# Packed attention and a channel mixer on one core: half of the packs are made between the mixer's products

## The chip, the cores and the metric

The kernel runs on one core of a Trainium2 chip. TensorE (PE) multiplies matrices and writes its results to PSUM; VectorE (DVE), ScalarE (ACT) and GpSimd (POOL) work elementwise; SyncE (SP) issues all transfers of this kernel. Each engine takes its instructions from its own queue, in order, and waits on semaphores for the others. The metric is the time of one execution in microseconds (us); lower is better.

## The reference

There are 8 batches of 8 heads with 576 tokens and 64 channels. Each head has 32 learned "pack" queries `p`. First the packs attend to the tokens, then the tokens attend to the packs:

```python
p_packed = sm_attn(p, k, v)              # 32 x 64 per head: "the packs"
x = sm_attn(q, p_packed, p_packed)       # 576 x 64 per head
# heads side by side: x is (8, 576, 512)
u = x + (x.transpose(0, 2, 1) @ U @ V).transpose(0, 2, 1)
out = u + np.maximum(u @ w_ch1, 0) @ w_ch2
```

`sm_attn` is a softmax attention with scale 1/8, the row maximum subtracted and 1e-9 added to the sum. `U` (576 x 32), `V`, `w_ch1` (512 x 2048) and `w_ch2` (2048 x 512) come as 64-bit floats, everything else as 32-bit.

## The kernel before

**Numbers.** A float32 matrix is split into a high part and a rest (`fp32r` tiles with names that end in h and l, or hi and lo), and three products stand for one (`mm3`, L74 to L78). `float32_of` (L67 to L71) turns 64-bit words into float32: one ACT and four VectorE instructions on a 128 x 512 tile.

**The packs are folded into w1.** Since the packs of a batch are the values of the second attention, `u @ w1` becomes "attention weights times (packs @ w1)". The products packs @ w1 are written to DRAM (`wsr` for batches 0 to 3, `wsc` for batches 4 to 7) and read back in pieces of 256 columns (`load_wt`, `split_wt`).

**First stage.** A unit is one batch and half of its heads (four). For all 16 units, in rounds (the loop over `i`, L479), the kernel loads k, v and p, turns k with VectorE (`a_split`, the 128 x 1152 transposition of L101) and p into a block-diagonal tile `bdp`, multiplies (`a_scores`), takes the maximum over all 576 tokens and the exponential (`a_softmax`), turns the weights with TensorE (`a_turn`) and multiplies them with v (`a_pack`): one product per 128 tokens, 128 rows (4 heads x 32 packs) by 256 columns (4 heads x 64), of which only the four diagonal blocks are used; ScalarE scales these by the reciprocal of the sum into `ppall`. In the same rounds `some_w1` converts and splits the 16 chunks of w1, `a_pairs` and `fold` make the products of batches 0 to 3 with w1, and steps of `attention(0)` are taken. A planner sets the order of the instructions in this stage, by program order and by what is ready. After the loop come the remaining folds, the rest of `attention(0)`, the first pieces of folded weights, the first chunk of w2, and the first two steps of `attention(1)`.

**The batches.** From L531 on the order is as written. For each batch b and each of 16 column blocks kt (NK = 16, 128 columns each): `gemm1(kt)` (12 products into `h_ps0` and `h_ps1`; ScalarE writes relu into `hh` and `hjh`, VectorE the rests `hl` and `hjl`), then `gemm2(kt - 1)` (12 products into the four `o` tiles), then at even kt `load_wt` and `split_wt`, in batch 0 `split_w2`, `load_w2` and `convert_w2`, then from batch 1 on the steps of `later`, which fold batches 4 to 7 into `wsc` (`twice` and `heads` turn their packs, `load`, `convert`, `split_heads`, `product` handle one chunk of w1), and then one step of the list `steps`, the second attention of the batch that follows. `h_ps0` and `h_ps1` have one buffer each: the next `gemm1` waits until `hl` and `hjl` are written. Each pair of batches has a joint product for its last 64 tokens (`joint`).

**Second attention.** `attention(b, res)` is a list of 16 steps, one per kt: `blocks` writes the packs into the block-diagonal tile `bdq` (L167) and splits it into `bqh` (ACT, L170) and `bql` (POOL, L171); `turn_q` and `split_q` turn and split q (`nat`, `natT`, `nhi`, `nlo`, one buffer each); then scores, softmax, `tokens` (into two `vt` buffers), `mix1` and `mix2`. Its first step is taken at kt 12 two batches ahead of its own, the others one per kt in the batch ahead of its own. PSUM for all this, and for `heads` and `product`, is the pool `psT` with two buffers.

The change and the prediction touch the first stage's units (L288 to L379, the loop at L479), `attention` (L157), `later` (L551) and the loop over batches (from L687).

Of the kernel before, what the change touches and what calls it, by code (L numbers as in the profile page):

```python
# [8 lines left out]
F32 = mybir.dt.float32  # L9
F32R = mybir.dt.float32r  # L10
I32 = mybir.dt.int32
AF = mybir.ActivationFunctionType
ALU = mybir.AluOpType
AX = mybir.AxisListType
# [5 lines left out]
def packed_attention_mixer_kernel(  # L20
# [23 lines left out]
    nc = tc.nc  # L44
    B, H, S, D = q.shape
# [4 lines left out]
    P = 128  # L50
    NB = S // 32
    SM = 512
    NK = DF // P
    NU = 2 * B
# [217 lines left out]

    res = {}
# [11 lines left out]
    UN = [(b, g) for b in range(B) for g in range(2)]  # L285
    ua = {}
# [8 lines left out]

    def a_load_v(u):
        b, g = UN[u]
        gh = slice(4 * g, 4 * g + 4)
        vt = pipe.tile([P, 5, 4 * D], F32, name="vt", tag="vt", bufs=2)
        nc.sync.dma_start(out=vt[:, :4].rearrange("p h x -> p (h x)").rearrange("p (h x) -> p h x", h=4),  # L300
                          in_=v[b, gh, :SM].rearrange("h (p k) d -> p h (k d)", k=4))
        nc.sync.dma_start(out=vt[:64, 4].rearrange("p (h d) -> p h d", h=4),
                          in_=v[b, gh, SM:].rearrange("h p d -> p h d"))
        ua[u]["v"] = vt
# [47 lines left out]
    def a_pack(u):  # L352
# [10 lines left out]
        if b < B // 2:  # L363
            ua[u]["twice"] = sA.tile([P, 2, D], F32, name="twice", bufs=1)
            nc.scalar.copy(ua[u]["twice"], ppall[:, b, g].unsqueeze(1).to_broadcast([P, 2, D]))
# [95 lines left out]
    a_load_v(0)  # L461
# [17 lines left out]
    for i in range(NU + 3):  # L479
# [4 lines left out]
        if i + 1 < NU:  # L484
            a_load_v(i + 1)
# [4 lines left out]
        if i > 1:  # L490
            some_w1()
        if i < NU:
            a_softmax(i)
        if i >= 5 and first and i not in (16, 17):
            first.pop(0)()
# [5 lines left out]
        if 0 <= i - 3 < NU // 2:  # L501
            a_pairs(i - 3)
        if 6 < i < 13:
            some_w1()
# [21 lines left out]
    for _ in range(2):  # L526
        steps.pop(0)()
# [162 lines left out]
    folds[0][0]()  # L690
    folds[0][1]()
    for b in range(B):
# [3 lines left out]
        for kt in range(NK):  # L696
# [3 lines left out]
            if done and kt % 2 == 0 and kt > 0:  # L700
                pr, cc = done.pop(0)
                folds[pr][5](cc)
# [20 lines left out]
            if b > 0 and kt > 0:  # L723
# [5 lines left out]
                elif kt % 2 == 1:  # L729
# [6 lines left out]
                    if rest and kt < NK - 1:  # L736
                        pr, cc = rest.pop(0)
                        folds[pr][2](cc)
                        held.append((pr, cc))
            if steps:  # L740
                steps.pop(0)()
            if kt == 1:
                cur.blocks()
# [41 lines left out]
```

## Time and profile before

| | us |
|---|---|
| median of 3 runs (lowest, highest) | 874.68 (874.37, 875.54) |
| the profiled execution | 876.01 |
| its span, first to last instruction | 874.2 |
| TensorE busy in the span | 826.7 (95%) |
| VectorE busy | 512.6 (59%) |
| ScalarE busy | 374.0 (43%) |
| GpSimd busy | 258.6 (30%) |
| read from and written to DRAM | 71.5 and 26.2 MB, 112 GB/s over the span |

In a row of groups stand: line, engine, operation, output <- inputs (buffer numbers left out), shapes and count, then busy time in us and the mean of one in ns, then the idle time of the engine just before these instructions and who ended it. A row of waits gives the engine and line that waited, whom it waited for, the sum in us, the count and the longest. A row of the timeline gives the start, the duration, the instruction and in brackets the idle time before it. Matmuls are pipelined: the duration of one overlaps the next, so the spacing of their starts is what one costs.

### The profile page before, as it was taken

Reading aid. Unit: us, or ns where it says so; the run is one execution under the profiler, and the core shown is the slowest. Engines: PE = TensorE matmul, PEld = TensorE weight load, DVE = VectorE, ACT = ScalarE, POOL = GpSimd, SP = SyncE. Lnnn points to the kernel's source line nnn. Section 1 sums busy time; section 2 is a strip of 40 time slices with the busy share of each in tenths; the row PEclk is TensorE's granted clock in tenths of the full one; section 3 lists DMA queues with packets and bytes.
Section 4 is the critical chain, followed back from the end, with each engine's and each line's share of the span. In section 5 each row is a group of like instructions: output and inputs, shape, how many; then the busy total and the mean of one; then the engine's idle time right before and its main releaser. Section 6 shows DMA issues by size and latency. Waiting matters only on the chain.

```text
span 874.2 us, 12574 instructions
## 1 busy us (share of the span) xinstructions
PE 826.7 (95%) x4440; PEld 706.8 (81%) x4440; DVE 512.6 (59%) x1032; ACT 374.0 (43%) x960; POOL 258.6 (30%) x230
## 2 busy tenths in 40 slices
PE   4779889988989999999999999999999999999997
PEld 2557666777879888888888888988888889889886
DVE  7999985889857876478676433443543424432220
ACT  2557576534445554455554332233333322333220
POOL 3302353545343313132233232323242313221110
PEclk9989997999999999999999999999999999999999
DMA  9869775723424444334453103010301120002001
GB/s 318 236 204 330 221 222 187 253 85 121 160 64 123 140 144 130 98 112 126 117 182 85 53 13 112 25 60 17 112 25 63 56 70 25 25 14 95 25 1 60
DMA packets 59998, 98.55 MB, mean 113 GB/s; under 512 B 12192, under 2 KB 36768, under 8 KB 59936
## 3 DMA queue, kind: packets, MB, share of 16 engines
q1 hardware_dynamic: 59936, 97.75, 36.0%
q8 instruction: 35, 0.57, 0.3%
q14 instruction: 27, 0.22, 0.1%
HBM read 71.52 MB, written 26.21 MB: 112 GB/s over the span
## 4 chain that ended last, share of the span: by engine, by line
PE 73%; DVE 17%; DMA 4%; ACT 3%; issue 3%; SPq 0%; POOL 0%; DVEq 0%; ACTq 0%; POOLq 0%
PE o L78 14%; PE o L77 14%; PE o L76 14%; PE h_ps L76 7%; PE h_ps L77 7%; PE h_ps L78 7%; DVE kT L101 3%; DVE os L70 2%; DVE natT L101 2%; DVE os L69 2%; DMA bits<-in_moe_w_ch_dram 2%; PE w_ps L592 2%; DVE os L71 2%; DVE os L68 2%; PE s_ps L322 2%
## 5 line engine op out<-in xcount | busy, mean ns | idle before, releaser
L640 DVE SCALAR_TENSOR_TENSOR hl<-h_ps,hh 128x256 fp32r<-128x256 f32 x256 | 104.1, 418 | 181.1 <-ACT hh L638 145.7
L78 PE MATMUL o<-w2h,hl 128*128 128x512 f32 x512 | 202.1, 395 | 0.0
L76 PE MATMUL o<-w2h,hh 128*128 128x512 f32 x512 | 201.3, 393 | 0.0
L77 PE MATMUL o<-w2l,hh 128*128 128x512 f32 x512 | 200.9, 392 | 0.0
L638 ACT ACTIVATE hh<-h_ps 128x256 fp32r<-128x256 f32 x256 | 96.0, 383 | 234.4 <-PE h_ps L78 231.4
L76 PE MATMUL h_ps<-ah,fold 128*128 128x256 f32 x496 | 149.3, 301 | 6.3 <-DVE hl L640 5.9
L453 POOL TENSOR_TENSOR fold<-fold 128x512 fp32r<-128x512 f32 x62 | 81.2, 1310 | 230.1 <-ACT fold L452 222.6
L77 PE MATMUL h_ps<-al,fold 128*128 128x256 f32 x496 | 146.1, 295 | 0.0
L78 PE MATMUL h_ps<-ah,fold 128*128 128x256 f32 x496 | 145.7, 294 | 0.0
L78 PEld LDWEIGHTS o<-w2h,hl 128*128 128x128 f32 x512 | 96.4, 188 | 21.6
L77 PEld LDWEIGHTS o<-w2l,hh 128*128 128x128 f32 x512 | 96.6, 189 | 17.5
L76 PEld LDWEIGHTS o<-w2h,hh 128*128 128x128 f32 x512 | 96.7, 189 | 16.8
L76 PEld LDWEIGHTS h_ps<-ah,fold 128*128 128x128 f32 x496 | 93.5, 188 | 13.4 <-DVE hl L640 10.3
L77 PEld LDWEIGHTS h_ps<-al,fold 128*128 128x128 f32 x496 | 93.5, 189 | 2.1
L78 PEld LDWEIGHTS h_ps<-ah,fold 128*128 128x128 f32 x496 | 93.3, 188 | 0.0
L181 POOL TENSOR_TENSOR nlo<-natT,nhi 128x576 fp32r<-128x576 f32 x32 | 46.0, 1453 | 115.5 <-ACT nhi L180 115.5
L68 DVE TENSOR_SCALAR os<-os 128x512 f32<-128x512 f32 (+2 forms) x51 | 37.1, 727 | 40.0 <-ACT os L67 39.9
L322 PE MATMUL s_ps<-kT,bdp 128*128 128x288 f32 x128 | 39.3, 457 | 9.4 <-DVE bdp L313 9.2
L180 ACT CAST nhi<-natT 128x576 fp32r<-128x576 f32 x32 | 20.7, 675 | 55.8 <-DVE natT L101 48.6
L124 POOL TENSOR_TENSOR w1l<-os,w1h 128x512 fp32r<-128x512 f32 x16 | 21.4, 1337 | 67.7 <-ACT w1h L123 61.1
L101 DVE STREAM_TRANSPOSE kT<-nat 128x1152 f32<-128x1152 f32 x16 | 37.3, 2329 | 5.7 <-DMA nat<-in_k_dram 5.6
L67 ACT ACTIVATE os<-bits 128x512 f32<-128x512 f32 x48 | 32.3, 674 | 18.9 <-DMA bits<-in_moe_w_ch_dram 14.7
(143 smaller groups left out, 1398.5 us busy)
## 6 DMA issues: line engine op xcount, KB each, us to landing
bits<-in_moe_w_ch_dram SPq DMA_DIRECT2D x48, 512.0 KB, 4.3
nat<-in_k_dram SPq DMA_DIRECT2D x16, 576.0 KB, 5.3
nat<-in_q_dram SPq DMA_DIRECT2D x16, 576.0 KB, 4.4
vt<-in_v_dram SPq DMA_DIRECT2D x16, 512.0 KB, 5.6
wsr<-fold SPq DMA_DIRECT2D x32, 256.0 KB, 3.8
out_dram<-bits SPq DMA_DIRECT2D x16, 512.0 KB, 3.0
wsc<-bits SPq DMA_DIRECT2D x64, 128.0 KB, 2.2
fold<-wsc SPq DMA_DIRECT2D x32, 256.0 KB, 2.8
```

The lines of the kernel that those rows point to most:

```text
L67: nc.scalar.activation(t, high.bitcast(F32), AF.Abs)
L68: nc.vector.tensor_single_scalar(t, t, LEAST, op=ALU.max)
L76: nc.tensor.matmul(ps, lhsT=lh, rhs=rh, start=start, stop=False)
L77: nc.tensor.matmul(ps, lhsT=lh, rhs=rl, start=False, stop=False)
L78: nc.tensor.matmul(ps, lhsT=ll, rhs=rh, start=False, stop=stop)
L101: nc.vector.transpose(t.rearrange("p h (i c) -> p c h i", c=NB), nat.rearrange("p (c h l) -> p c h l", h=2, l=32),)
L124: nc.gpsimd.tensor_tensor(lo, x, hi.bitcast(F32), op=ALU.subtract)
L181: nc.gpsimd.tensor_tensor(lo[:, dh], t, hi[:, dh].bitcast(F32), op=ALU.subtract)
L322: nc.tensor.matmul(s_ps[:, hf, :288], lhsT=bdp[b % 2][:, 2 * g + dh], rhs=kT[:, dh, 288 * hf:288 * hf + 288], start=dh == 0, stop=dh == 1)
L453: nc.gpsimd.tensor_tensor(lo, raw, hi.bitcast(F32), op=ALU.subtract)
L638: nc.scalar.activation(hi, src, AF.Relu)
L640: nc.vector.scalar_tensor_tensor(lo, src, 0.0, hi.bitcast(F32), op0=ALU.max, op1=ALU.subtract)
```

## The change

Eight of the 16 units stay in the first stage: those of batches 0 to 3 (`NU = B`). The loop has 11 rounds in place of 19; `some_w1` runs in each round, twice from the fifth on. One step of `attention(1)`, not two, is taken ahead of the batches.

The eight units of batches 4 to 7 become `packs(b, g)`, seven steps each: `L` loads p and k, `V` loads v, `T` scales p (POOL) and turns k (VectorE), `A` and `B` make the scores of 288 tokens each, `X` turns the weights back with TensorE and `P` multiplies with v. They use tiles of the second attention: `nat`, `natT`, `nlo` (for the exponentials), `nhi` (for the turned weights), `vt`, two of the four slots of `bdq`, and `psT`. Since the scores come in halves, the maximum runs: the first half's exponentials are taken with the first maximum, and rescaled by POOL once the second is known. `P` makes for each of 5 token blocks and 4 heads one product with 32 output rows and 64 columns, each head into its own 32 partitions of `pp_ps`, and one ScalarE instruction writes all heads to `ppall`.

`plan` says where each step stands: (kt, z, steps, unit), z = 0 behind `gemm1`, z = 1 behind `convert_w2`, z = 2 behind the step of `attention`. Batches 0 and 1 take three units each, batch 2 two. The order is half g = 0 of batches 4 to 7, then g = 1. The folds of batches 4 to 7 start 14 column blocks later (at kt 13 of batch 1) and are no longer left out at kt 0 and kt 15.

```diff
-    NU = 2 * B
+    NU = B
...
+    def packs(b, g):
+        st = {}
+        bdk = bdq[:, 2 * g:2 * g + 2]
...
+        def turn():
+            nc.gpsimd.tensor_scalar_mul(st["p"], st["p"], scale)
+            st["t"] = transposed(pipe.tile([P, 2, S], F32, name="natT", bufs=1), st["nat"])
+
+        def scores(hf):
+            if hf == 0:
+                for h in range(4):
+                    hs = slice(32 * h, 32 * h + 32)
+                    nc.vector.transpose(bdk[hs, :, hs], st["p"][hs].rearrange("p (e l) -> p e l", l=32))
+                st["e"] = pipe.tile([P, 2, S // 2], F32, name="ke", tag="nlo", bufs=1)
...
+            e, m, sm = st["e"], st["m"], st["s"]
+            s_ps = psT.tile([P, 512], F32, name="s_ps", tag="t")
+            for dh in range(2):
+                nc.tensor.matmul(s_ps[:, :288], lhsT=bdk[:, dh], rhs=st["t"][:, dh, 288 * hf:288 * hf + 288],
+                                 start=dh == 0, stop=dh == 1)
+            mx = m[:, hf:hf + 1]
+            nc.vector.tensor_reduce(mx, s_ps[:, :288], axis=AX.X, op=ALU.max, negate=True)
+            if hf == 1:
+                nc.vector.tensor_tensor(mx, mx, m[:, :1], op=ALU.min)
+            nc.scalar.activation(e[:, hf], s_ps[:, :288], AF.Exp, bias=mx, accum_out=sm[:, hf:hf + 1])
+            if hf == 1:
+                nc.scalar.activation(sm[:, 2:3], m[:, :1], AF.Exp, scale=-1.0, bias=mx)
+                nc.gpsimd.tensor_scalar_mul(e[:, 0], e[:, 0], sm[:, 2:3])
+                nc.vector.scalar_tensor_tensor(sm[:, 3:], sm[:, :1], sm[:, 2:3], sm[:, 1:2], op0=ALU.mult, op1=ALU.add)
+                nc.vector.tensor_scalar_add(sm[:, 3:], sm[:, 3:], 1e-9)
+                nc.vector.reciprocal(sm[:, 3:], sm[:, 3:])
+
+        def turn_back():
...
+            for kk in range(4):
+                nc.tensor.transpose(t_ps[:, kk], ec[:, kk], ident)
+            nc.tensor.transpose(t2_ps[:64, :P], e[:, SM:], ident)
+            eT = st["eT"] = pipe.tile([P, 5, P], F32, name="keT", tag="nhi", bufs=1)
+            nc.scalar.copy(eT[:, :4], t_ps)
+            nc.vector.tensor_copy(eT[:64, 4], t2_ps[:64, :P])
+
+        def pack():
...
+            for kk in range(5):
+                rows = P if kk < 4 else 64
+                for h in range(4):
+                    hs = slice(32 * h, 32 * h + 32)
+                    rhs = vm[:, kk, h] if kk < 4 else vt[:rows, 4, D * h:D * h + D]
+                    nc.tensor.matmul(pp_ps[hs, :D], lhsT=eT[:rows, kk, hs], rhs=rhs, start=kk == 0, stop=kk == 4)
+            nc.scalar.activation(ppall[:, b, g], pp_ps[:, :D], AF.Copy, scale=st["s"][:, 3:])
...
-        if i > 1:
-            some_w1()
+        some_w1()
...
-        if 6 < i < 13:
+        if i > 3:
             some_w1()
...
     steps = attention(1, res)
-    for _ in range(2):
-        steps.pop(0)()
+    steps.pop(0)()
...
-    folds[0][0]()
-    folds[0][1]()
+
+    units = [packs(b, g) for g in range(2) for b in range(B // 2, B)]
+    units = [units[:3], units[3:6], units[6:]]
+
+    plan = ((5, 1, "LV", 0), (6, 1, "T", 0), (6, 1, "L", 1), (8, 0, "A", 0), (8, 1, "B", 0), (9, 0, "T", 1),
+            (9, 0, "L", 2), (9, 1, "X", 0), (10, 0, "P", 0), (10, 1, "A", 1), (11, 0, "B", 1), (11, 1, "T", 2),
+            (12, 0, "X", 1), (12, 2, "V", 1), (12, 2, "V", 2), (13, 0, "A", 2), (13, 1, "B", 2), (14, 0, "P", 1),
+            (14, 1, "X", 2), (15, 1, "P", 2))
...
             cur.gemm1(kt)
...
+            place(b, kt, 0)
+            if done and kt % 2 == 0:
...
                     w2x = convert_w2(kt + 2)
-            if b > 0 and kt > 0:
+            place(b, kt, 1)
+            if b * NK + kt == NK + 13:
+                folds[0][0]()
+            if b * NK + kt == NK + 14:
+                folds[0][1]()
+            if b * NK + kt > NK + 14:
...
             if steps:
                 steps.pop(0)()
+            place(b, kt, 2)
```

56 lines of the change are left out of this document (37 added, 19 removed).

## The prediction

> **What bounds the kernel now.** I read the page's spans and chain first, then the busy time by stage, then the waits of TensorE, then the groups of the first stage, and last the instructions in order of time around one `gemm1`. The chain that ended last and the busy time cut at the stage borders (columns: window, length, then busy us and instructions of PE, PEld, DVE, ACT, POOL, then granted clock, DMA share, GB/s):
>
> ```profile
> PE 73%; DVE 17%; DMA 4%; ACT 3%; issue 3%; SPq 0%; POOL 0%; DVEq 0%; ACTq 0%; POOLq 0%
> ```
>
> ```profile
> 0.00:10.00 10.00, 0.84 (x2) 0.73 (x3) 4.32 (x6) 1.97 (x2) 4.45 (x14) 1.00 0.78 262
> 10.00:125.00 115.00, 97.06 (x405) 71.78 (x405) 109.01 (x197) 69.23 (x182) 34.15 (x30) 0.94 0.82 256
> 125.00:162.60 37.60, 31.65 (x120) 21.48 (x119) 23.80 (x43) 22.81 (x52) 17.77 (x20) 0.86 0.69 216
> 162.60:250.00 87.40, 78.71 (x433) 68.17 (x432) 74.62 (x136) 42.11 (x103) 42.05 (x33) 0.96 0.38 125
> 250.00:338.00 88.00, 87.68 (x498) 77.04 (x497) 63.57 (x125) 46.05 (x112) 25.95 (x22) 1.00 0.43 128
> 338.00:426.00 88.00, 87.52 (x492) 76.64 (x491) 58.60 (x111) 42.98 (x101) 20.44 (x17) 1.00 0.42 120
> 426.00:874.20 448.20, 443.30 (x2501) 390.96 (x2499) 178.72 (x418) 148.89 (x412) 113.80 (x96) 1.00 0.18 57
> ```
>
> The reader is to see two bounds. From 10 to 125 us VectorE works 109.01 of 115 us: the first stage is VectorE's. The first `gemm1` product starts at 162.6 us, and from there TensorE has work nearly all the time (87.68 of 88.00 in the second batch). Only batch 0 (162.6 to 250) leaves it 8.7 us idle, and its waits say why: VectorE, busy 85% with `convert_w2`, comes late with `hl`.
>
> ```profile
> PE h_ps L76 <- DVE hl L640: 8.5, 7, 2.3
> ```
>
> So the change takes eight packs out of a stage that VectorE bounds and puts them into one that TensorE bounds. Each pack has a price on both sides.
>
> **What the first stage loses.** VectorE's groups from 0 to 162.6 us that a pack uses, per unit and per batch:
>
> ```profile
> L101 DVE STREAM_TRANSPOSE kT<-nat 128x1152 f32<-128x1152 f32 x16 | 37.3, 2329 | 5.7 <-DMA nat<-in_k_dram 5.6
> L330 DVE TENSOR_REDUCE mx<-s_ps 128x1 f32<-128x576 f32 x16 | 12.0, 747 | 0.3
> L313 DVE STREAM_TRANSPOSE bdp<-pn 32x128 f32<-32x128 f32 x32 | 9.5, 295 | 0.4
> L68 DVE TENSOR_SCALAR os<-os 128x512 f32<-128x512 f32 x18 | 9.1, 504 | 10.8 <-ACT os L67 10.8
> L101 DVE STREAM_TRANSPOSE natT<-nat 128x1152 f32<-128x1152 f32 x3 | 7.0, 2335 | 0.1
> L350 DVE RECIPROCAL sm<-sm 128x1 f32<-128x1 f32 x16 | 2.5, 156 | 0.2
> L349 DVE TENSOR_SCALAR sm<-sm 128x1 f32<-128x1 f32 x16 | 2.3, 144 | 0.6 <-ACT e L332 0.5
> ```
>
> One unit: 2.33 + 0.75 + 2 x 0.295 + 0.16 + 0.14 = 3.97 us; eight make 31.8. The second step of `attention(1)` (one `natT` transpose, 2.33) also leaves, since one step fewer is taken before the batches: 34.1 us. VectorE's idle 13.8 us from 125 to 162.6 I leave as it is; it belongs to the last chunks of w1, the folds and the end of `attention(0)`, none of which gets shorter. I take 34.1, so the first `gemm1` starts near 128.5. It is a good deal less certain than it looks. The low end: the 16 chunks of w1, spread over rounds 2 to 12 of 19 before, now come in rounds 0 to 9 of 11, two in a round from the fifth on; their first VectorE instruction (L68) already waited 10.8 us in sum for ACT, and if that doubles, 23 us are saved. The high end is VectorE's work itself: 4.32 (before 10 us) + 109.01 + 23.80 = 137.1 busy, minus 34.1 is 103.0, after a first 5.6 us without work: 108.6, or 54 us saved.
>
> **What TensorE gets.** The same instructions, in warm stretches, as it does them today (start, us, instructions; a float32 product is recorded as two):
>
> ```profile
> 22.96 2.11 PE L322 MATMUL s_ps<-kT,bdp 128*128 128x288 f32 x8
> 24.91 1.89 PE L358 MATMUL pp_ps<-vt,eT 128*128 128x256 f32 x8
> 159.17 0.60 PE L562 MATMUL z_ps<-ident,os 128*128 128x128 f32 x4
> 159.53 0.47 PE L76 MATMUL w_ps<-w1h,lwh 128*128 128x512 f32 x1
> ```
>
> Scores: the same eight records, 2.11 us, only split over two places. `turn_back`: five transposes; four took 0.36 (159.17 to 159.53), 0.09 each, so 0.45. `pack` is new in form: 20 products of 32 output rows and 64 columns, 40 records, where 10 of 256 columns stood. No row shows a column tile. The nearest is `pp_ps`: 1.89 / 8 = 236 ns for 256 columns, 59 ns for 64, and 40 of them in a row make 2.36. Low end: four heads abreast, ten times 59 ns, 0.59. High end: 40 at the 90 ns of the transposes, the closest-spaced float32 instructions here, 3.6. I take 2.36, the row's own rate. Sum per unit 2.11 + 0.45 + 2.36 = 4.92, eight units 39.4 us. TensorE has no free time in batches 1 and 2 to hide it. In batch 0 the 8.7 idle us are waits for VectorE, and VectorE gets work too: per unit 2.33 + 4 x 0.295 + two half reductions of 0.37 + four column operations of 0.15 (minimum, sum, 1e-9, reciprocal) + the 64-row copy into `keT`, which I estimate at 0.3; 5.2, three times, and the 2.33 of the moved step: 74.6 + 17.9 = 92.5 in a batch that becomes some 108 long. That is the same 85%, so I leave those waits as they are.
>
> **The waits that are new.** At (8, 0) the plan puts scores A straight after `gemm1(8)` on TensorE. Its `bdk` transposes stand in VectorE's queue behind the two `hl` and the `hjl` of that same `gemm1`. An undisturbed `gemm1`:
>
> ```profile
> 520.32 0.28 PE L76 MATMUL h_ps<-ah,fold 128*128 128x256 f32 x1
> ...
> 521.76 0.31 PE L78 MATMUL h_ps<-ah,fold 128*128 128x320 f32 x1
> 521.90 0.39 PE L76 MATMUL o<-w2h,hh 128*128 128x512 f32 x1
> 522.98 0.21 DVE L640 SCALAR_TENSOR_TENSOR hjl<-h_ps,hjh 128x64 fp32r<-128x64 f32 x1
> ```
>
> ```profile
> 17.21 1.23 DVE L313 STREAM_TRANSPOSE bdp<-pn 32x128 f32<-32x128 f32 x4
> ```
>
> TensorE is free at 521.90, `hjl` ends at 523.19, four transposes take 1.23: TensorE waits 2.5 us, and `gemm2(7)`, next in its queue, waits behind it. That is unit 0 in batches 0, 1 and 2: 7.5. At (13, 0), unit 2 of batches 0 and 1, it is longer: `blocks()` of the next `attention` writes the same `bdq` at kt 12, and `bdk` may be overwritten only when POOL has read it for `bql`. The chain starts with `mix1`, the last TensorE work of kt 12:
>
> ```profile
> 231.34 0.28 PE L236 MATMUL m_ps<-tl,ua 64*128 64x256 f32 x1
> 231.54 0.39 PE L76 MATMUL h_ps<-ah,fold 128*128 128x256 f32 x1
> 231.65 0.37 ACT L239 CAST ms<-m_ps 128x256 fp32r<-128x256 f32 x1 [2.35 <-PE m_ps L236]
> 232.41 0.42 DVE L240 TENSOR_TENSOR ms<-m_ps,ms 32x256 fp32r<-32x256 f32 x1
> ```
>
> ```profile
> 239.69 1.24 DVE L167 STREAM_TRANSPOSE bdq<-ppall 32x128 f32<-32x128 f32 x4
> 240.96 0.62 ACT L170 CAST bqh<-bdq 128x512 fp32r<-128x512 f32 x1 [0.73 <-DVE bdq L167]
> 241.66 1.28 POOL L171 TENSOR_TENSOR bql<-bdq,bqh 128x512 fp32r<-128x512 f32 x1
> ```
>
> From 231.54: 0.11 + 0.37 + 0.42 + 1.24 + 0.62 + 1.28, and 1.23 for `bdk`, is 5.3, against a `gemm1` of 1.58 (the twelve products before 521.90 began at 520.32): 3.7 idle, twice, 7.4. Unit 1's A, at (10, 1), comes behind `gemm2(9)`, when `hl` is long done: nothing. The waits sum to 14.9. Low end 0, if VectorE should reach `bdk` ahead; high end in the rivals.
>
> **What is covered.** Each unit brings one load of k and two of v and one of p to SP's queue:
>
> ```profile
> nat<-in_k_dram SPq DMA_DIRECT2D x16, 576.0 KB, 5.3
> vt<-in_v_dram SPq DMA_DIRECT2D x16, 512.0 KB, 5.6
> vt<-in_v_dram SPq DMA_DIRECT2D x16, 64.0 KB, 5.4
> ```
>
> Load and use of k are at least one kt apart (5.5 us: 88 us over 16), of v more; the DMA engines stand at 0.38 to 0.43 in these batches. If a k load landed late, VectorE would stop at `T` with `hl` behind it, up to 5.3 us each. SP waits at (12, 2) until `mix1` frees `vt`; behind it are the q load, used four kt later, and `load_wt` of kt 14, whose piece is split two kt later. POOL (42 of 87 us) takes the scaling of p and of `e`, ACT (42) two exponentials and copies; both have room. `A` to `X` is a whole kt, `X` to `P` a `gemm1`. The folds start 14 kt later, in the same number; their last column chunk is written at batch 4, kt 0, and first read at kt 8 or after (`load_wt` at kt 8 for columns from 1536). They cost nothing more.
>
> **Sum.** -34.1 + 39.4 + 14.9 = +20.2. The profiled execution took 876.01 (span 874.2, 1.8 outside it), 1.3 above the median 874.68; on it 896.2, on the median 895.
>
> **The rivals.** *Column tiles run abreast.* The four heads write four separate strips; if they overlap, `pack` costs 0.59 and not 2.36: -14.2, 881. For it: neighbours in the queue never share a strip. Against it: no row shows two products overlapping for less than one's time. The Trainium skill, "TensorEngine Tiling (Array Packing)", Tiling Modes, states that different tiles load weights and multiply in parallel, and that changing the mode drains the engine; no run so far shows either, and by it this rival would hold. 30%.
>
> *The first stage goes by rounds (faster).* If the planner's order lets each round cost its 7.8 us (125 / 16) whatever else is in it, eight rounds less save 62 and not 34: 867. It decides once the first `gemm1` starts before 106.5 us (34.1 + 20.2 + 1.7 earlier than 162.6). For it: the transfers share was 0.82 and TensorE's clock 0.94 there. Against it: VectorE was busy 95% and cannot end before 108.6 unless its instructions get shorter as well. 12%.
>
> *The new waits cost more.* After a wait of 2.31 us TensorE ran at about half pace here:
>
> ```profile
> 178.21 0.58 PE L76 MATMUL h_ps<-ah,wt 128*128 128x256 f32 x1 [2.31 <-DVE hl L640]
> 181.26 0.41 PE L76 MATMUL o<-w2h,hh 128*128 128x512 f32 x1
> ```
>
> That `gemm1` took 3.05 us against 1.58. Five waits with such a tail add 7.4: 902. 18%. With w1 late in the first stage (23 saved): 906. 7%.
>
> **How the numbers follow.** My forecast, 895, has 33% (its own range 889 to 900). The range is 877 to 908: it takes in the abreast case with some room and the late ones, and leaves out the faster rival and the tails. Within 0.2% (1.7 us, about what a measurement of this kernel tells from no change) falls only what lies between the abreast case and the faster rival: 3%. Faster 12%, slower 85%.
>
> **What would show it.** Right: the first `gemm1` near 128 us; 40 `pp_ps` records per unit about 59 ns apart; five waits of TensorE for `bdk` of 2.5 to 3.7 us; batches 1 and 2 longer by 15 to 22 us, from batch 3 on as before. Wrong: `pp_ps` within 1 us per unit; no wait named `bdk`; a first stage that ends before 110 or after 140.

## The result, and the profile after

The changed kernel takes 945.62 us (median of 4 runs, 938.93 to 947.57), the kernel before, run beside it, 874.52 (869.86 to 875.54): a ratio of 1.081, 95% interval 1.075 to 1.088. It is 71 us slower, where 20 were forecast. The spans of the profiled executions are 944.4 and 874.2 us.

Both spans are cut at the same seven places: the first `gemm1`, then the first copy of each batch's results into `bits` (the end of its products), up to batch 3. Columns: window, length, then busy us and instructions of PE, PEld, DVE, ACT and POOL, then granted clock, DMA share and GB/s. The kernel before, busy time by window:

```profile
0.00:162.62 162.62, 129.56 (x524) 93.99 (x525) 137.12 (x244) 94.03 (x235) 56.38 (x64) 0.93 0.79 247
162.62:256.06 93.44, 84.75 (x464) 73.47 (x463) 76.52 (x141) 44.06 (x109) 43.56 (x34) 0.96 0.36 117
256.06:341.64 85.58, 85.26 (x485) 74.86 (x484) 64.87 (x127) 46.91 (x113) 25.31 (x21) 1.00 0.44 131
341.64:441.56 99.92, 99.25 (x553) 86.66 (x552) 66.38 (x127) 50.08 (x118) 25.30 (x21) 1.00 0.41 120
441.56:523.48 81.92, 81.79 (x469) 72.40 (x468) 43.30 (x96) 34.42 (x90) 25.18 (x21) 1.00 0.28 86
523.48:874.20 350.72, 346.14 (x1950) 305.43 (x1948) 124.45 (x299) 104.54 (x296) 82.89 (x69) 1.00 0.15 49
```

The changed kernel, the same view:

```profile
0.00:137.54 137.54, 95.09 (x336) 66.18 (x337) 112.76 (x195) 71.64 (x169) 52.38 (x59) 0.85 0.69 218
137.54:269.73 132.19, 102.88 (x623) 85.81 (x622) 91.81 (x177) 49.94 (x130) 48.51 (x41) 0.92 0.37 113
269.73:372.65 102.92, 94.71 (x620) 80.46 (x619) 49.76 (x120) 34.63 (x101) 28.97 (x27) 0.97 0.28 83
372.65:494.69 122.04, 115.02 (x680) 96.76 (x678) 77.31 (x157) 55.73 (x137) 28.09 (x25) 0.97 0.43 127
494.69:591.48 96.79, 89.00 (x475) 76.84 (x476) 70.16 (x133) 51.60 (x121) 25.25 (x21) 0.95 0.41 122
591.48:944.40 352.92, 348.27 (x1950) 304.03 (x1948) 124.57 (x299) 104.57 (x296) 82.58 (x69) 1.00 0.16 50
```

The first stage is 25.1 us shorter. The batches 0 to 3 are longer by 38.8, 17.3, 22.1 and 14.9, the rest by 2.2; the sum is 70.2, the difference of the spans. In batches 0 to 3 TensorE sat idle for 9.8 us before (length less busy, four rows) and sits idle for 52.3 after: 29.3, 8.2, 7.0 and 7.8. Its granted clock there was 0.96 to 1.00 and is 0.92 to 0.97.

Who ends these waits, from the first `gemm1` to the end of batch 2 (waits of TensorE in the changed kernel: engine, line, releaser, sum in us, times, longest):

```profile
PE s_ps L310 <- DVE bdq L303: 18.4, 6, 3.7
PE h_ps L76 <- DVE hl L704: 10.4, 8, 3.2
PE t_ps L330 <- DVE tl L228: 4.9, 2, 3.8
PE v_ps L249 <- ACT ke L316: 3.8, 2, 2.6
PE pp_ps L345 <- DVE keT L334: 3.1, 2, 2.7
```

All of a pack's steps on TensorE are in this list: the scores (`s_ps`) wait for `bdk`, the turn (`t_ps`) and the product (`pp_ps`) for VectorE, and work that is not the pack's (`h_ps`, `v_ps`) waits too. One such wait from batch 0 shows how it comes about. The timeline of VectorE in the changed kernel (start, us, instruction):

```profile
226.87 0.43 DVE L68 TENSOR_SCALAR os<-os 128x512 f32<-128x512 f32 x1 [0.48 <-ACT os L67]
227.40 1.32 DVE L69 TENSOR_SCALAR os<-os 128x512 int32<-128x512 int32 x1
228.76 0.69 DVE L70 SCALAR_TENSOR_TENSOR os<-bits,os 128x512 int32<-128x512 int32 x1
229.49 0.69 DVE L71 SCALAR_TENSOR_TENSOR os<-bits,os 128x512 int32<-128x512 int32 x1
230.10 2.33 DVE L101 STREAM_TRANSPOSE natT<-nat 128x1152 f32<-128x1152 f32 x1
232.27 1.00 DVE L228 TENSOR_TENSOR tl<-t_ps,th 128x512 fp32r<-128x512 f32 x2
```

The timeline of TensorE at the same time:

```profile
233.09 1.10 PE L330 MATMUL t_ps<-ident,ke 128*128 128x128 f32 x4 [3.82 <-DVE tl L228]
...
234.06 0.78 PE L76 MATMUL o<-w2h,hh 128*128 128x512 f32 x1
234.63 0.63 PE L77 MATMUL o<-w2l,hh 128*128 128x512 f32 x1
235.06 0.63 PE L78 MATMUL o<-w2h,hl 128*128 128x512 f32 x1
...
237.12 0.40 PE L76 MATMUL o<-w2h,hh 128*128 128x512 f32 x1
237.35 0.39 PE L77 MATMUL o<-w2l,hh 128*128 128x512 f32 x1
```

Step `X` of unit 1 stands right behind a `gemm1`. It needs a buffer of `psT`, and that buffer is free only when VectorE has read the second attention's `t_ps` into `tl`. VectorE has first to convert a chunk of w2 (L68 to L71) and to turn the k of unit 2 (step `T`, 2.33 us, placed one step earlier in the plan). So TensorE waits 3.82 us, with `gemm2` behind it in its queue. Then it starts slowly: `gemm2`'s products stand 0.43 us apart at first (234.63, 235.06) and 0.23 later (237.12, 237.35). This wait is paid once as idle time and once more as slow work behind it. Most long waits have such a tail, but not all: after the 3.60 us for `bdk` at 244.72, `gemm2`'s products stood 0.23 us apart from the second on.

### The profile page after: what moved, and what is told of

Read it like the earlier page. It is cut to its first block, busy times and chain, and to the rows that moved or that the text cites. A ratio compares the mean times of both kernels' runs of the same rounds, so it can differ in the third digit from the quotient of the medians.

```text
span 944.4 us, 13107 instructions
## 1 busy us (share of the span) xinstructions
PE 845.0 (89%) x4680; PEld 710.1 (75%) x4680; DVE 526.4 (56%) x1080; ACT 368.1 (39%) x952; POOL 265.8 (28%) x242
## 4 chain that ended last, share of the span: by engine, by line
PE 58%; DVE 3%; ACT 1%; issue 1%; DMA 0%; ACTq 0%; DVEq 0%; SPq 0%
PE o L76 12%; PE o L77 12%; PE o L78 12%; PE h_ps L76 5%; PE h_ps L77 5%; PE h_ps L78 5%; PE w_ps L656 2%; PE s_ps L310 1%; PE m_ps L236 1%; DVE natT L101 1%; PE s_ps L76 1%; PE s_ps L78 1%; PE s_ps L77 1%; PE t_ps L225 0%; PE v_ps L249 0%
## 5 line engine op out<-in xcount | busy, mean ns | idle before, releaser
L76 PE MATMUL o<-w2h,hh 128*128 128x512 f32 x512 | 208.3, 407 | 2.7 <-ACT bits L723 2.7
L77 PE MATMUL o<-w2l,hh 128*128 128x512 f32 x512 | 204.6, 400 | 0.0
L78 PE MATMUL o<-w2h,hl 128*128 128x512 f32 x512 | 204.3, 399 | 0.0
L519 POOL TENSOR_TENSOR fold<-fold 128x512 fp32r<-128x512 f32 x62 | 80.2, 1294 | 258.3 <-ACT fold L518 249.8
L76 PEld LDWEIGHTS h_ps<-ah,fold 128*128 128x128 f32 x496 | 94.1, 190 | 16.8 <-DVE hl L704 13.3
L68 DVE TENSOR_SCALAR os<-os 128x512 f32<-128x512 f32 (+2 forms) x51 | 38.0, 745 | 41.2 <-ACT os L67 41.2
L101 DVE STREAM_TRANSPOSE natT<-nat 128x1152 f32<-128x1152 f32 x24 | 55.7, 2323 | 0.1
L67 ACT ACTIVATE os<-bits 128x512 f32<-128x512 f32 x48 | 32.2, 672 | 21.8 <-DMA bits<-in_moe_w_ch_dram 20.8
L70 DVE SCALAR_TENSOR_TENSOR os<-bits,os 128x512 int32<-128x512 int32 x48 | 39.5, 822 | 1.4
L518 ACT CAST fold<-fold 128x512 fp32r<-128x512 f32 x62 | 38.6, 623 | 0.1
```

What stands on the lines that cost most here:

```text
L67: nc.scalar.activation(t, high.bitcast(F32), AF.Abs)
L68: nc.vector.tensor_single_scalar(t, t, LEAST, op=ALU.max)
L70: nc.vector.scalar_tensor_tensor(x, high, -0x40000000, x, op0=ALU.bitwise_and, op1=ALU.bitwise_or)
L76: nc.tensor.matmul(ps, lhsT=lh, rhs=rh, start=start, stop=False)
L77: nc.tensor.matmul(ps, lhsT=lh, rhs=rl, start=False, stop=False)
L78: nc.tensor.matmul(ps, lhsT=ll, rhs=rh, start=False, stop=stop)
```

## The experiments

Each experiment is an edit of the changed kernel unless it says otherwise, and each ratio is taken against runs of the kernel before on the same chip (869 to 877 us).

**1. Own tiles for `bdk`.** `bdk` leaves `bdq`, and its transposes move from `A` to `T`:

```diff
-        bdk = bdq[:, 2 * g:2 * g + 2]
+        bdk = bdk2[(b + 4 * g) % 2]
```

> The block-diagonal tiles of the moved packs are their own (two tiles in place of slots of bdq), and their four transposes stand at step T, two column blocks ahead of A. Theory (the waits for bdk and the slow clock behind each are the largest part of the loss): the six waits of TensorE for bdq in scores A, 18.4 us in the trace of the changed kernel, go, and with each some 1.5 us of slow clock: 918 us. Rival (the wait moves on to the next step, X or P, because VectorE is late anyway): at most 8 us less, 937 us.

Measured: 935.36 (933.35 to 935.65), ratio 1.070 (1.065 to 1.075). That is nearer the rival's 937 than the theory's 918. No wait names `bdk` any more; 18.4 us of waits are gone, and 10 us of time. The rest came back under other names (waits of TensorE in this run, first `gemm1` to the end of batch 2):

```profile
PE h_ps L76 <- DVE hl L707: 11.3, 8, 3.2
PE t_ps L333 <- DVE tl L231: 8.3, 3, 5.2
PE pp_ps L348 <- DVE keT L337: 5.5, 3, 3.7
```

So the place of `bdk` in `bdq` and behind `A` was where VectorE's lateness was first met, and only in part its cause.

**2. One k load later.** In batch 0 SyncE waits for `nat` behind the load at (9, 0), with a w2 load behind it. The load moves to (9, 1):

```diff
-            (9, 0, "L", 2), (9, 1, "X", 0), (10, 0, "P", 0), (10, 1, "A", 1), (11, 0, "B", 1), (11, 1, "T", 2),
+            (9, 1, "L", 2), (9, 1, "X", 0), (10, 0, "P", 0), (10, 1, "A", 1), (11, 0, "B", 1), (11, 1, "T", 2),
```

> Only the load of the third unit is moved, from (9, 0) to (9, 1), behind load_w2 in SP's queue. Theory (SP stands 14.5 us at that load, waiting for the buffer nat; the w2 chunk behind it comes late, and with it convert_w2 and the bdk transposes queued behind it): the wait at (10, 1) goes, 3 to 6 us less, 941 us. Rival (SP's queue is what makes batch 0 longer, 36 us): 15 to 20 us less, 927 us.

Measured: 945.23 (940.51 to 948.77), ratio 1.081 (1.076 to 1.087). Nothing changed; both expectations missed. SyncE's wait for `nat` that stood at 14.5 us fell to 5.5, and TensorE's six waits for `bdk` stayed (17.2 us, 18.4 before the edit). So the place of this load is not what costs; the rest of SyncE's queue was left as it was.

**3. No fold work at the batch edges.** The change had let the folds of batches 4 to 7 run at kt 0 and kt 15 as well. Here they leave these out again and start two column blocks earlier:

```diff
-            if done and kt % 2 == 0:
+            if done and kt % 2 == 0 and (kt > 0 or b == B // 2):
...
-            if b * NK + kt > NK + 14:
+            if b * NK + kt > NK + 12:
...
-                    if rest:
+                    if rest and kt < NK - 1:
```

> The folds of batches 4 to 7 skip the ends of a batch again: no chunk of w1 is loaded at kt 15, no product at kt 0 but in batch 4, and to end in time they start two column blocks earlier. Theory (the stores at a batch's end share the two buffers bits with these chunks; one store waits 3 us for the other, and the next gemm1 5 us): batch 3, 96.5 us long, loses 8 to 10, 936 us. Rival (these waits lie beside other work): no change, 945 us.

Measured: 934.3 (932.29 to 936.85), ratio 1.069 (1.065 to 1.074); 11 us come back, as the theory had it. Batch 3 falls from 96.79 to 87.85 us, batch 2 from 122.04 to 118.11. In the changed kernel the edge from batch 2 to batch 3 looks like this (timeline of TensorE):

```profile
499.00 0.80 PE L76 MATMUL o<-w2h,hh 128*128 128x512 f32 x1 [2.12 <-ACT bits L723]
...
506.95 0.58 PE L76 MATMUL h_ps<-ah,fold 128*128 128x256 f32 x1 [5.02 <-DVE hl L704]
```

At an edge the results leave through the two `bits` buffers. A chunk of w1 that is loaded at kt 15 holds one of them, so the stores take turns, the `o` tiles come free late, and VectorE, which empties them, is late with `hl`.

**4. No packs in the batches.** The plan is empty and the packs of batches 4 to 7 are zeros:

```diff
-        for k2, z2, which, u in plan:
+        for k2, z2, which, u in ():
```

> The moved packs are left out altogether: no step of the plan is issued, and the packs of batches 4 to 7 are zeros. All the rest is the changed kernel. It gives the price of the packs in the batches, and what the first stage gains. Theory (first stage 25 us shorter, edges of the batches 8 to 10 us longer): 860 us, so that the packs between the products cost 85 us. Rival (the late folds and the moved step of attention cost more than that): 870 us or more.

Measured: 863.69 (862.91 to 864.26), ratio 0.988 (0.985 to 0.992), nearer the theory's 860 than the rival's 870. The packs in the batches cost 82 us. Busy time by window, batches 0 to 3:

```profile
136.57:230.97 94.40, 84.72 (x464) 73.63 (x463) 79.33 (x142) 44.09 (x109) 44.61 (x35) 0.96 0.36 122
230.97:311.49 80.52, 79.60 (x461) 70.54 (x460) 35.98 (x85) 28.50 (x80) 25.11 (x21) 1.00 0.20 61
311.49:414.63 103.14, 102.90 (x574) 89.87 (x572) 70.39 (x133) 52.01 (x123) 25.26 (x21) 1.00 0.44 127
414.63:510.29 95.66, 86.54 (x475) 75.57 (x476) 70.15 (x133) 51.45 (x121) 25.26 (x21) 0.96 0.43 123
```

and the sum over batches 4 to 6 (510.29 to 771.91 us), for the experiments that follow:

```profile
sum 261.62, PE 261.49 PEld 231.61 DVE 105.81 ACT 84.14 POOL 73.83; mean PE 87.16 PEld 77.20 DVE 35.27 ACT 28.05 POOL 24.61
```

Against the kernel before, batches 0 to 3 are 373.72 instead of 360.86 us long: 12.9 us is the price of the moved folds and of the step of `attention(1)` that now lies in batch 0, most of it idle time (20.0 against 9.8). By batch it is +1.0, -5.1, +3.2 and +13.7, so batch 3 has all of it, and batch 1 got shorter by the folds that left it. Against the changed kernel (453.94) they are 80.2 shorter: the price of the packs, 10.0 a unit.

**5. The same plan in batches 4 to 6**, where no w2 is converted and, but for the last one at the start of batch 4, no fold is made. The folds still use zeros for batches 4 to 7.

```diff
-    units = [units[:3], units[3:6], units[6:]]
+    units = [[], [], [], [], units[:3], units[3:6], units[6:]]
```

> The same plan of the same eight packs, but in batches 4 to 6, where VectorE has no w2 and almost no folds beside it (busy 40% before). The folds read zeros in place of the packs of batches 4 to 7. Without any packs this kernel takes 863.7, with them in batches 0 to 2 945.6: 82 us for eight, of which TensorE's own work is 8 x 3.15 = 25. Theory (more than half of the rest is VectorE and ScalarE being late with w2 and the folds): only the waits for bdk and their slow clock stay, some 20 us, so 25 + 20 more than without packs, 909 us. Rival (the chain of steps is too tight in itself): again about 80 us, 940 us.

Measured: 920.46 (917.99 to 921.47), ratio 1.054 (1.050 to 1.057), between the two expectations. The sum of the busy times of batches 4 to 6 (513.59 to 829.95 us):

```profile
sum 316.36, PE 299.60 PEld 256.45 DVE 142.47 ACT 100.56 POOL 84.39; mean PE 99.87 PEld 85.48 DVE 47.49 ACT 33.52 POOL 28.13
```

These three batches are 54.7 us longer than in experiment 4, 6.8 a unit. So 25.5 of the 80.2 us came from lying in batches 0 to 3, beside the w2 conversions and the folds; but even with VectorE busy less than half the time (142.47 of 316.36) the plan makes TensorE wait, 16.8 us, where without packs it waited 0.1.

**6. A plan with more room.** Own `bdk`, the fold edges of experiment 3, the small copy into `keT` on ScalarE, and a plan in which `T` of the next unit no longer stands ahead of `X` and more time lies between the steps:

```diff
-            nc.vector.tensor_copy(eT[:64, 4], t2_ps[:64, :P])
+            nc.scalar.copy(eT[:64, 4], t2_ps[:64, :P])
...
-    plan = ((5, 1, "LV", 0), (6, 1, "T", 0), (6, 1, "L", 1), (8, 0, "A", 0), (8, 1, "B", 0), (9, 0, "T", 1),
-            (9, 0, "L", 2), (9, 1, "X", 0), (10, 0, "P", 0), (10, 1, "A", 1), (11, 0, "B", 1), (11, 1, "T", 2),
-            (12, 0, "X", 1), (12, 2, "V", 1), (12, 2, "V", 2), (13, 0, "A", 2), (13, 1, "B", 2), (14, 0, "P", 1),
-            (14, 1, "X", 2), (15, 1, "P", 2))
+    plan = ((4, 1, "LV", 0), (5, 1, "T", 0), (6, 1, "L", 1), (8, 0, "A", 0), (8, 1, "B", 0), (9, 1, "X", 0),
+            (9, 1, "T", 1), (9, 1, "L", 2), (10, 0, "P", 0), (10, 1, "A", 1), (11, 0, "B", 1), (11, 2, "T", 2),
+            (12, 2, "X", 1), (12, 2, "V", 1), (12, 2, "V", 2), (13, 0, "A", 2), (14, 0, "B", 2), (14, 1, "P", 1),
+            (15, 0, "X", 2), (15, 1, "P", 2))
```

> Own block-diagonal tiles and the folds that skip the ends of a batch, as in the runs before, and a plan with more room: the first k load and T one column block earlier, T of the second and third unit behind the steps whose VectorE work they delayed, X of the second unit behind mix1, B, P and X of the third half a column block later, and the 64-row copy of the turned weights on ScalarE. Theory (the loss is waits of TensorE, and each can be moved away from): the 16 us of waits for keT, tl and ke that own tiles left, with 1.5 us of slow clock each, go as well as the edges' 11: 935 - 11 - 27 = 897 us. Rival (VectorE is full in batch 0 and a wait only moves): 920 us.

Measured: 914.26 (912.73 to 916.04), ratio 1.047 (1.043 to 1.051): it missed the theory's 897 and lies nearer the rival's 920. Batches 0 to 2 are 117.85, 93.46 and 121.02 us long. Batch 1, which has no w2 and hardly a fold beside the packs, pays 12.9 us for three units against experiment 4; batch 0 still pays 23.5 and batch 2 some 18, for two units and folds that start two blocks earlier.

**7. `P` as row products**, five products of 128 rows and 256 columns, as the first stage makes them, instead of 20 column tiles:

```diff
-                for h in range(4):
-                    hs = slice(32 * h, 32 * h + 32)
-                    rhs = vm[:, kk, h] if kk < 4 else vt[:rows, 4, D * h:D * h + D]
-                    nc.tensor.matmul(pp_ps[hs, :D], lhsT=eT[:rows, kk, hs], rhs=rhs, start=kk == 0, stop=kk == 4)
+                rhs = vm[:, kk] if kk < 4 else vt[:64, 4].rearrange("p (h d) -> p h d", h=4)
+                nc.tensor.matmul(pp_ps, lhsT=eT[:rows, kk], rhs=rhs, start=kk == 0, stop=kk == 4)
```

> P in the form of the first stage: one product of 128 rows and 256 columns per token block in place of four column tiles of 64 columns, and four ScalarE instructions on the diagonal blocks. Column tiles took 0.83 us of TensorE per unit in the trace. Theory (the four strips overlap): the row form costs 10 x 0.2 = 2.0 to 2.4 us, so 8 x 1.2 to 1.6 more, 957 us. Rival (the step waits anyway, and the column form saves nothing): 946 us.

Measured: 956.95 (956.46 to 958.42), ratio 1.096 (1.093 to 1.100): 11 us slower, 1.4 a unit, as the theory had it. The column tiles do run abreast. An undisturbed `P` of the changed kernel, 40 records, with what follows, and then the same `P` in this run, ten records:

```profile
368.53 0.90 PE L345 MATMUL pp_ps<-vt,keT 128*32 128x64 f32 x40
369.36 0.38 PE L76 MATMUL h_ps<-ah,fold 128*128 128x256 f32 x1
```

```profile
376.05 2.52 PE L343 MATMUL pp_ps<-vt,keT 128*128 128x256 f32 x10
378.50 0.38 PE L76 MATMUL h_ps<-ah,fold 128*128 128x256 f32 x1
```

The 40 records take 0.83 us, 21 ns each; the ten that make the same product in full rows take 2.45. That different tiles multiply in parallel is what the Trainium skill states ("TensorEngine Tiling (Array Packing)", Tiling Modes); the trace agrees.

**8. w1 earlier in the first stage**: two chunks a round from the second round on.

```diff
-        if i > 3:
+        if i > 0:
             some_w1()
```

> Two chunks of w1 per round from the second round of the first stage on, not from the fifth. Theory (the first stage ends with the last chunk of w1: its conversion began at 114.8 us, 138.5 before, and the first gemm1 followed 23 to 24 us later both times): the first gemm1 comes 5 to 10 us earlier, 938 us. Rival (VectorE's work bounds it, whatever the order): no change, 945 us.

Measured: 950.81 (948.51 to 955.06), ratio 1.088 (1.084 to 1.092): slower, which neither expectation had, and the first `gemm1` at 141.2 us. VectorE was busy 117.9 us up to there (112.8 in the changed kernel). Taking w1 earlier doesn't help, so its place late in the rounds doesn't look like what kept the first stage from the forecast.

**9. The clean price of a pack.** Experiment 5 with own `bdk`, the copy on ScalarE and the plan of experiment 6.

> The eight packs stand in batches 4 to 6 as in the run with the plan moved there, but with their own bdk tiles, the plan with more time between the steps, and the copy into keT on ScalarE; batches 4 to 7 are again folded with zeros, so the output is not the reference's. Compared with the run that leaves the packs out (863.7 us). Theory: with the waits of the plan gone, what is left is TensorE's own work, 3.2 us of bare spacing and some 0.8 us at the changes between float32 and fp32r steps, 4.0 a unit, so 32 us: 895. Rival 1: only the bare spacing counts, 25 us: 889. Rival 2: the waits of the plan come back in other places as they did in batches 0 and 2, and it stays near the 920.5 of the first plan in these batches: 910 or more.

Measured: 891.46 (890.21 to 891.77), ratio 1.021 (1.017 to 1.025). The first `gemm1` came at 129.97 us here, 6.6 earlier than in experiment 4, so the total says less than the batches do. The sum of the busy times of batches 4 to 6 (505.41 to 799.69 us):

```profile
sum 294.28, PE 293.07 PEld 252.83 DVE 139.80 ACT 102.33 POOL 84.17; mean PE 97.69 PEld 84.28 DVE 46.60 ACT 34.11 POOL 28.06
```

They are 294.28 us long, 32.7 more than without packs: 4.1 a unit, as the theory had it, and TensorE idles 1.2 us in all. Against experiment 5 (316.36 long, 299.60 busy) 22.1 us are gone: 15.6 of idle time and 6.5 of busy time, for the same 1,913 products. The 6.5 is TensorE working slowly behind its waits; the granted clock goes from 0.98 to 1.00. Two times half a unit's scores with what follows, timeline of TensorE in this run:

```profile
652.39 1.14 PE L314 MATMUL s_ps<-natT,bdk 128*128 128x288 f32 x4
653.15 0.50 PE L76 MATMUL h_ps<-ah,fold 128*128 128x256 f32 x1
653.49 0.28 PE L77 MATMUL h_ps<-al,fold 128*128 128x256 f32 x1
653.61 0.28 PE L78 MATMUL h_ps<-ah,fold 128*128 128x256 f32 x1
```

```profile
663.74 1.14 PE L314 MATMUL s_ps<-natT,bdk 128*128 128x288 f32 x4
664.71 0.60 PE L229 MATMUL t_ps<-ident,aT 128*128 128x128 f32 x4
```

The first of these seems to say 0.76 us for half the scores and 0.2 us for the change from float32 to `fp32r`, since the product behind them holds TensorE for 0.34 us (653.15 to 653.49) and the next for 0.12. But the four records stand 0.24 us apart, and that product's record begins only 0.03 us after the fourth: its 0.34 us hold the fourth's time too (0.03 + 0.34 is 0.24 + 0.12, rounding aside). Where another float32 step follows, at 663.74, half the scores take their 0.97 us. So the scores of a unit cost 1.94 us, and these rows show no price of the change of format.

**10. Column tiles in the kernel before**, in `a_pack` of the first stage, with one ScalarE instruction for the scaling in place of four:

```diff
-            nc.tensor.matmul(pp_ps, lhsT=eT[:, kk], rhs=vm[:, kk], start=kk == 0, stop=False)
...
+                nc.tensor.matmul(pp_ps[hs, :D], lhsT=eT[:rows, kk, hs], rhs=rhs, start=kk == 0, stop=kk == 4)
+        nc.scalar.activation(ppall[:, b, g], pp_ps[:, :D], AF.Copy, scale=rs)
```

> The kernel before, with one thing of the change: a_pack of the first stage makes its product in column tiles (20 products of 32 rows and 64 columns, one ScalarE instruction for the scaling in place of four). Theory: the first stage is bound by VectorE, whose work is the same; TensorE's 1.0 us a unit less (1.89 to 0.83) is not on the path: 874, within 1 us. Rival: VectorE's 10.8 us of waits for ScalarE's L67 come from ScalarE's crowded queue, and three instructions fewer a unit take a good part of them away: 868 to 870.

Measured: 878.6 (877.55 to 880.73), ratio 1.0066 (1.0042 to 1.0090). TensorE has less to do, and the kernel is 5 us slower; neither expectation has that. VectorE's waits for L67 did fall, from 10.8 to 4.1 us, but nothing was won by it: the first `gemm1` comes at 166.2, and the batches are as before. VectorE was busy 141.2 us up to 165, 4.1 more than before up to 162.6, with the same work: the four groups L68 to L71 of 128 x 512 take 53.5 us (49.2 before), L70 alone 1,018 ns in the mean (781). Experiment 11 shows one thing that stretches them; why they are stretched more here was not looked into. VectorE bounds that stage, so the 3.6 us of the first `gemm1` are put down to this; no run tests it.

**11. No low part of w1**: the 16 GpSimd subtractions of `split_w1` are left out of the changed kernel.

```diff
-        split(x, w1t[pr][0][:, cs], w1t[pr][1][:, cs])
+        nc.scalar.copy(w1t[pr][0][:, cs], x)
```

> The changed kernel without the 16 GpSimd subtractions that make the low part of w1 in the first stage (21.5 us of GpSimd); the folds of batches 0 to 3 take the high part in its place, so the output is not the reference's. Theory: the first stage fell short of its forecast because VectorE's conversions of w1 run beside GpSimd and are stretched (L70 991 ns in the mean after, 781 before, 0.67 alone); without those subtractions the four groups L68 to L71 lose 4 to 8 of their 54.4 us and the first gemm1 comes 4 to 8 us earlier: 938 to 942. Rival: the stretch has another cause, the four groups stay at 54 us and the time at 945.

Measured: 939.18 (929.92 to 940.5), ratio 1.073 (1.069 to 1.078). The first `gemm1` comes at 126.4 us, 11.1 earlier. The sum of the busy times up to there, in this run:

```profile
sum 126.40, PE 86.29 PEld 62.31 DVE 103.38 ACT 71.69 POOL 30.15; mean PE 43.15 PEld 31.16 DVE 51.69 ACT 35.84 POOL 15.07
```

VectorE was busy 103.4 us instead of 112.8. Its groups of the first stage in the changed kernel (line, shapes, count, busy us, mean ns, idle before):

```profile
L70 DVE SCALAR_TENSOR_TENSOR os<-bits,os 128x512 int32<-128x512 int32 x18 | 17.8, 991 | 0.3
L68 DVE TENSOR_SCALAR os<-os 128x512 f32<-128x512 f32 x18 | 10.9, 604 | 6.2 <-ACT os L67 6.2
```

and without the subtractions:

```profile
L70 DVE SCALAR_TENSOR_TENSOR os<-bits,os 128x512 int32<-128x512 int32 x18 | 14.0, 775 | 0.2
L68 DVE TENSOR_SCALAR os<-os 128x512 f32<-128x512 f32 x18 | 8.0, 447 | 6.9 <-ACT os L67 6.6
```

L69 falls from 12.5 to 9.7 us as well, and L71 rises from 13.2 to 15.6; the four groups together fall from 54.4 to 47.3, within the 4 to 8 of the theory. So GpSimd's work does stretch VectorE's. Of the 11.1 us only some 6 reach the end: batch 0 is 137.0 us long here, 4.8 more.

**12. Four packs instead of eight**, with the edits of experiment 6: batches 0 to 5 stay in the first stage.

```diff
-    NU = B
+    NU = 12
...
-    units = [units[:3], units[3:6], units[6:]]
+    units = [units[:1], units[1:3], units[3:]]
```

> The replanned version (own bdk tiles, folds away from the edges, keT copied by ScalarE, the plan with more time between its steps) with four packs moved instead of eight: batches 0 to 5 stay in the first stage, and one unit is made in batch 0, two in batch 1, one in batch 2. Theory: a unit saves 3.1 us in the first stage (25.1 / 8) and costs at least its 4.0 us of TensorE, so no number of packs moved pays; with the prices of the replanned version (7.8 in batch 0, 4.3 in batch 1, 9 in batch 2) four cost 25 and save 12.5 and the rest of the change adds some 3: 890 (885 to 895). Rival: packs that do not crowd a batch cost little, and it comes to 874 or below.

Measured: 890.88 (889.64 to 891.84), ratio 1.020 (1.017 to 1.024). It lies between the kernel before and experiment 6 (914.26), with the first `gemm1` at 146.1. The expected 890 was met in part by luck: both sides of its sum are larger, with the first `gemm1` 16.6 us earlier than before (12.5 expected) and all that follows 32.5 longer (28 expected). Of all versions that compute the reference, the kernel before remains the fastest.

## Why the prediction was wrong

The direction was right, by the mechanism named: packs leave a stage bound by VectorE and enter one bound by TensorE. The size was not: 895 forecast, 877 to 908 as the range, 945.6 measured. The 70.2 us between the spans, by cause (TensorE's own work is taken over from the batches 4 to 6 of experiment 9, and the slow work is what is then left of the growth of TensorE's busy time in batches 0 to 3):

| | forecast | measured | from |
|---|---|---|---|
| first stage | -34.1 | -25.1 | spans before and after |
| TensorE's own work | +39.4 | +31.6 | busy time, experiment 9 less 4 |
| TensorE idle beside the packs | +14.9 | +32.4 | idle, batches 0 to 3, after less experiment 4 |
| TensorE slow behind its waits | 0 | +16.3 | busy 401.6 less 353.8, less 31.6 |
| the moved folds | 0 | +12.9 | batches 0 to 3, experiment 4 less before |
| the rest | 0 | +2.2 | span from batch 4 on |

**The step that failed** is the sum of TensorE's waits, in "The waits that are new", together with "that is the same 85%, so I leave those waits as they are". The five waits it listed were there and of the right size: six waits for `bdk` sum to 18.4 us, and without the one at (10, 1) to 15.4, against 14.9. That one the prediction had at nothing; it took 2.97:

```profile
220.02 1.24 PE L310 MATMUL s_ps<-natT,bdq 128*128 128x288 f32 x4 [2.97 <-DVE bdq L303]
```

The amount of VectorE's work in batch 0 was also foreseen (92.5, measured 91.81); its share was not, since the batch became 132 us long and not 108 (69%). All idle time beside the packs came to 32.4 us, not 14.9. What was missing is that not its share but its place counts: each step of a pack is a short chain between TensorE and VectorE, put directly behind a product, and whatever VectorE has in its queue just then (a w2 chunk of 3.2 us, a transposition of 2.33) is waited for in full. The change also uses `psT`, with its two buffers, for the scores, the turn and the product of each pack, so that the second attention's `tl` and the packs hold each other up; the prediction did not speak of that. Experiments 5 and 9 show that the tight plan, the shared `bdq` and VectorE's copy into `keT`, with VectorE busy less than half the time, cost 22.1 us for eight units, idle and slow work together; experiment 1 shows that of 18.4 us of waits only 10 are won when they go.

**The slow work behind waits** was a rival ("The new waits cost more", 7.4 us for five waits). The mechanism is confirmed by experiments 5 and 9, where the same products take 6.5 us less once the waits are gone; with more and longer waits it came to 16.3 (what is left of TensorE's busy time when its own work is taken off) and was added to the idle time. It isn't behind every wait, as the one at 244.72 shows.

**"They cost nothing more"**, said of the folds, failed: their count is the same, but kt 0 and kt 15 belong to the stores. Experiment 3, which also starts the folds two column blocks earlier, gives 11 us back.

**The first stage** lost the work that was counted, and gained 25.1 us and not 34.1. The forecast took VectorE's durations from the kernel before as fixed (103.0 us busy to the first `gemm1`); VectorE's busy time came to 112.8, while its idle time stayed the same (24.8 of 137.54 us, 25.5 of 162.62 before). Two things make this difference of 9.8 us. The forecast added durations, but VectorE's records overlap (the transposition at 230.10 ends 0.16 us after the next instruction has begun): the durations summed to 148.7 us where VectorE was busy 137.1, and to 121.3 and 112.8 after, so 3.0 of the 9.8 are overlap that left with the instructions. The other 6.7 are instructions that took longer, 5.2 of them in L68 to L71 (49.2 us before, 54.4 after). In experiment 11 VectorE's busy time is 103.4 and the first `gemm1` comes at 126.4, near the 128.5 of the forecast: GpSimd beside the w1 conversions is worth that much. That it explains the growth is argued, not shown, since the kernel before had the same subtractions; in experiment 9, which has them too, the first `gemm1` came at 129.97. Experiment 8 speaks against w1 late in the rounds, which the prediction had named for the low end. The rival of rounds (first `gemm1` before 106.5) did not happen.

**TensorE's own work** was put too high, at 4.92 a unit, and is 3.95 (31.6 / 8). The term that was mis-sized is `P`: it runs abreast, 0.83 and not 2.36 us, the rival that had 30%. The scores were right within 0.2: 2.11 is the duration of eight pipelined records, of which the last overlaps what follows; from the first one's start to the next product's it is 1.95 (22.96 to 24.91), and 1.94 in experiment 9. With the scores at 1.94, 0.83 and the 0.45 of the turn, the steps come to 3.2; the other 0.7 of the 3.95 was not placed.

Of the signs the prediction named, the first `gemm1` near 128 and `pp_ps` 59 ns apart failed, the waits for `bdk` held, batch 1 held (17.3 longer), by luck, since its packs cost 22.4 (102.92 against 80.52 in experiment 4) and 5.1 went with the folds that left it, and batch 2 just missed (22.1 against 15 to 22), and "from batch 3 on as before" failed by 14.9.

A unit saved 25.1 / 8 = 3.1 us in the first stage of the changed kernel, and 4.1 where that stage ended earliest (32.7 / 8 in experiment 9, 16.6 / 4 in experiment 12). It costs 4.0 to 4.1 on TensorE even without waits. So at the best measured prices the two cancel, and the waits and the moved folds come on top. Whether a still better plan could win a little is not shown. Experiment 12 shows the middle of the way. What stays open is which part of the 25.5 us between batches 0 to 3 and quiet batches belongs to the w2 conversions and which to the folds, and why the first stage ended at 129.97 us in experiment 9 and between 136.6 and 137.6 in the changed kernel and in experiments 1 to 7, whose work there is the same.

## What to carry to other kernels

Before work is moved from a stage that one engine bounds to a stage that another bounds, compare the two prices of a unit without any wait: here 3.1 to 4.1 us saved against 4.0 to 4.1 paid left nothing to win. Then treat each step that is put into the bounding engine's queue as a wait for everything the helper engine has queued at that moment, and add slow work behind most waits; give such steps buffers of their own, and inputs that are ready a whole block earlier. Work at the edges of a loop shares buffers with the stores, so moving it there by one iteration isn't free.

## What the runs showed of the hardware

- TensorE often runs at about half pace behind a wait, for some 3 us (behind those at 346.57 and 506.95 for more than 5): after the 3.82 us shown in the section on the result, `gemm2`'s products stood 0.43 us apart and later 0.23, and after a wait of 2.73 us (at 212.38) just so until 3.1 us behind it. Of the 13 waits of 2 us or more in batches 0 to 2 and at the edge to batch 3, eight were followed by half pace at once, two within 1 us, and three not at all (2.97 us at 220.02, 3.60 at 244.72, 2.07 at 311.82). Length alone doesn't decide it.
- VectorE's w1 conversions can take four times as long beside a GpSimd instruction: in the timeline of the changed kernel L68 took 0.41 us with GpSimd idle and 1.63 beside it. The transpositions of k (2,331 ns in the mean of the changed kernel's first stage, 2,329 before) and the reductions of `s_ps` (754, 747) were not stretched.

```profile
72.04 0.41 DVE L68 TENSOR_SCALAR os<-os 128x512 f32<-128x512 f32 x1
...
84.56 1.85 POOL L181 TENSOR_TENSOR nlo<-natT,nhi 128x576 fp32r<-128x576 f32 x1
85.07 1.63 DVE L68 TENSOR_SCALAR os<-os 128x512 f32<-128x512 f32 x1
```

  The second L68 began 0.51 us after GpSimd's instruction and ended 0.29 after it, as if it had waited for its end. The Trainium skill ("SBUF — State Buffer", Who interferes with whom) says that the two engines share a pair of ports, that with some instructions, `tensor_scalar` among those that can, whichever engine issues first holds it for the whole instruction and that the other blocks; this row agrees, and experiment 11 shows the effect on the time.
- A float32 product in four column tiles of 32 output rows took 0.83 us where full rows took 2.45 (experiment 7).
- A float32 record of 128 x 288 costs 0.24 us; that of the last one can show up in the record of the product behind it (experiment 9), so the price of a step is read where another float32 step follows.
